# Softmax in slot-by-head rows, one accumulation for both outputs, and loads in order of use, in a fused attention and gated-MLP kernel

## The chip, the core and the metric

The kernel runs on one core of a Trainium2 chip. The metric is the device time of one launch in microseconds (us), as the median of several runs. A core has a matrix engine (TensorE, PE in the profile, with its weight loads listed apart as PEld), a vector engine (VectorE, DVE), a scalar engine (ScalarE, ACT) and a general engine (GpSimd, POOL). SyncE (SP) only issues transfers (DMAs). Each engine works through its own list of instructions in order, and engines wait for each other through semaphores. Matrix results go to PSUM, and other data lie in SBUF.

## The reference

One layer norm feeds two branches, which are added to the input. Sequence 2048, width 640, 32 heads of 20, and an attention window of 8 keys at distances 0, 2, ..., 14.

```
xn = layernorm(x)
q, k, v = split_heads(xn @ wqkv)                      # 640 -> 3*640
logits[s, w] = (q[s] . k[s - 2*w]) * scale            # w = 0..7, -1e9 where s - 2*w < 0
attn = softmax(logits, over w)
o[s] = sum_w attn[s, w] * v[s - 2*w]
out = x + o @ wo + ((xn @ w_gate) * (xn @ w_up)) @ w_down   # 640 -> 1536 -> 640
```

`wo` is the output projection. The softmax runs over eight slots per token and head. Data are bf16.

## The kernel before

The 2048 tokens are cut into four chunks of 512, and each chunk into four tiles of 128 tokens. In what follows "slot" is the window index w.

`proj_head(c)` (L153) loads the chunk's four x tiles from SP (L160), takes their statistics on DVE (`bn_stats` over five pieces of 128, L165; `bn_aggr`, L166), gets 1/std from one square root on ACT (L169) and one reciprocal on DVE (L172) for the whole chunk, and normalises each tile (L176). PE transposes each tile into `pst` (L186) and ACT copies it to `xnT_c` (L189). Then come 50 matmuls of 512 columns for q and k (L205, cast by ACT to `qT_c` and `kT_c`, L213 and L215) and 40 matmuls of 320 columns for v (L225, cast at L232). v goes to `vD` in DRAM (L233), since the window needs rows of v shifted against the partitions.

`prodlog(c)` (L238) makes the logits. DVE multiplies q with k shifted by 2w, one product `pw` per slot and half chunk (L250), and PE sums over the 20 features of each head with the 0/1 matrix `Ek`: 20 matmuls per group of four slots, placed side by side in the array, so that partition 32*j + h of `lps` holds slot j of head h (L259). ACT copies `lps` to `Lsb` in f32 (L268). `pw` has four buffers, so the next four products wait until PE has summed the last four.

`attn_core(c)` (L271) works tile by tile. It loads `v8`, eight shifted copies of v (L280), and transposes the logits to tokens-by-(slot, head) with two f32 PE transposes into `atp` (L283). Softmax follows in that layout: maximum (L299), difference (L302), exp on ACT (L305), sum (L307), reciprocal (L309), weight `a16` (L311). Then one large product `prod` = v8 * a16 (L316), a tree of three additions (L323, L325, L327) to `o16`, a transposition back (L330) and a copy to `oT_c` (L333). Tile 0 adds a mask first (L293 to L295).

`glu(c)` (L336) has 12 steps of 10 matmuls of 512 columns (L343, L352), two ACT casts (L360, L362) and one DVE product `hT_c` (L363). After them w_down gives `psB` (96 matmuls of 320 columns, L372), and DVE adds the residual x into `ob_c` (L379). `out_A(c)` (L387) multiplies `oT_c` with `wo` into `psA` (40 matmuls, L397), and DVE adds `ob_c` (L404) before the store from POOL's queue (L410).

All weights are loaded from POOL's queue: q and k first (L88), then v in five pieces whose buffers two ACT copies at a time must free (L94, L102), with the gate, up and down weights between them, and wo in 20 pieces (L143). The 10 first x tiles are issued by SP at the same time.

The program text runs projections of chunks 0 and 1, logits of chunk 0, and then per chunk: attention, GLU, projection of c+2, logits of c+1, output. A scheduler turns this text into one fixed list per engine, with instructions of neighbouring stages interleaved. The lists are fixed before the run, so an instruction whose input is late holds up everything behind it on its engine.

Of the kernel before, what the change touches and what calls it, by code (L numbers as in the profile page):

```python
# [15 lines left out]
def kernel(  # L16
# [35 lines left out]
    assert Dh % JL == 0 and Dh == JL * KT  # L52
    assert W * H == 2 * P

    TH = 256
    assert CS % TH == 0
    NTH = CS // TH

    if D <= 512:
        NSPL = [(0, D)]  # L60
    else:
        nspl = (D + 511) // 512
        assert D % nspl == 0
        NSPL = [(i * (D // nspl), D // nspl) for i in range(nspl)]

# [16 lines left out]
    wg = wpool.tile([P, KT, F], dt.bfloat16, name="wg")
    wu = wpool.tile([P, KT, F], dt.bfloat16, name="wu")
    wd = wpool.tile([P, FT, D], dt.bfloat16, name="wd")

    ident_bf = const.tile([P, P], dt.bfloat16, name="ident_bf")
    make_identity(nc, ident_bf[:])
    nc.gpsimd.dma_start(  # L88
        out=wqk[:], in_=A_wqkv[:, 0 : 2 * D].rearrange("(i p) f -> p i f", p=P)
    )  # L90
    st_tiles = []
    for i in range(KT):
        st = apool.tile([P, D], dt.bfloat16, name="st", tag="v8")
        nc.gpsimd.dma_start(  # L94
            out=st[:], in_=A_wqkv[i * P : (i + 1) * P, 2 * D : 3 * D]
        )
        st_tiles.append(st)
    nc.gpsimd.dma_start(out=wg[:], in_=B_w_gate.rearrange("(i p) f -> p i f", p=P))
    nc.gpsimd.dma_start(out=wu[:], in_=B_w_up.rearrange("(i p) f -> p i f", p=P))
    nc.gpsimd.dma_start(out=wd[:], in_=B_w_down.rearrange("(f p) d -> p f d", p=P))  # L100
    for i in range(KT):
        nc.scalar.copy(  # L102
            out=wvp[:, i, :].rearrange("p (j h) -> p j h", j=Dh, h=H),
            in_=st_tiles[i][:].rearrange("p (h j) -> p j h", h=H, j=Dh),
        )

    ident_f32 = const.tile([P, P], dt.float32, name="ident_f32")
    make_identity(nc, ident_f32[:])
    Ek = const.tile([P, KT, H], dt.bfloat16, name="Ek")
    for i in range(KT):  # L110
        et = apool.tile([P, D], dt.float32, name="et", tag="prod", bufs=1)
        nc.gpsimd.memset(et[:], 0.0)
        nc.gpsimd.tensor_copy(et[:, i * P : (i + 1) * P], ident_f32[:])
        e32 = apool.tile([P, H], dt.float32, name="e32", tag="m")
        nc.vector.reduce_sum(
            e32[:], et[:].rearrange("p (h j) -> p h j", h=H, j=Dh), AX.X
        )
        nc.vector.tensor_copy(Ek[:, i, :], e32[:])
# [34 lines left out]
    def proj_head(c):  # L153
# [3 lines left out]
        for ttl in range(CH):  # L157
# [6 lines left out]
            for g in range(KT):  # L164
                nc.vector.bn_stats(stats[:, g, :], x_t[:, g * P : (g + 1) * P])  # L165
# [288 lines left out]
```

## Time and profile before

| what | value |
|---|---|
| median of 6 runs | 332.79 us (331.89 to 334.89) |
| the profiled execution: its time | 333.7 us |
| its span (first to last instruction) | 331.9 us |
| granted PE clock, mean | 0.995 |
| transfers | 41.00 MB, 124 GB/s over the span |
| chain of waits, share by engine | DVE 31%, issue 26%, PE 22%, DMA 11%, ACT 5% |

How to read it: PE and DVE are the two loaded engines, and the chain of waits that ended last alternates between them. "Issue" is time in the chain in which the engine waited for nothing that the profile shows; here it stands mostly for PE or DVE working through its list while another engine's chain is followed. Matmuls are pipelined, so their busy time is not a pace: the pace of a group is the distance between the starts of two groups, divided by the count.

### The profile page before, as it was taken

What the parts mean: (1) busy time and instruction counts of PE and PEld (TensorE: products, weight loads), DVE (VectorE), ACT (ScalarE), POOL (GpSimd) and SP (SyncE); (2) the same over time, 40 slices, a digit from 0 to 9 for tenths busy, and PEclk for the clock granted to TensorE, in tenths of its full rate; (3) what the DMA queues carried; (4) which work ended last, traced back from release to release, by engine and by line L of the source; (5) the groups of instructions that cost most, each with busy time, mean ns of one, the idle gap of its engine ahead of it and who ended that gap; (6) DMA issues with size and microseconds to landing.
All of it is one profiled execution on the core that took longest, in us unless ns stands there. A gap on an engine that the chain in (4) does not pass through costs nothing.

```text
span 331.9 us, 5073 instructions
## 1 busy us (share of the span) xinstructions
PE 286.8 (86%) x1896; PEld 154.5 (47%) x1896; DVE 243.2 (73%) x452; ACT 134.0 (40%) x237; POOL 40.7 (12%) x84
## 2 busy tenths in 40 slices
PE   0139979799999889999999999999999799999990
PEld 0114544434446545544446646544446454445760
DVE  4352662678989895599889830798989797899861
ACT  1146654354651257245551255145541005553100
POOL 4022387000000100010000100010000111000111
PEclk9999999999999999999999999999999999999998
DMA  7828779310146625122346601115235711540011
GB/s 249 343 79 293 269 213 307 109 41 2 29 129 182 187 75 169 69 79 81 98 140 181 189 28 41 59 61 155 86 98 157 206 52 41 158 131 30 20 61 41
DMA packets 26922, 41.00 MB, mean 124 GB/s; under 512 B 3554, under 2 KB 24048, under 8 KB 26896
## 3 DMA queue, kind: packets, MB, share of 16 engines
q1 hardware_dynamic: 23040, 26.22, 25.9%
q0 software_dynamic: 3856, 14.44, 13.0%
q8 instruction: 15, 0.25, 0.3%
q14 instruction: 11, 0.09, 0.1%
HBM read 35.39 MB, written 5.26 MB: 122 GB/s over the span
## 4 chain that ended last, share of the span: by engine, by line
DVE 31%; issue 26%; PE 22%; DMA 11%; ACT 5%; POOL 2%; SPq 1%; POOLq 0%; DVEq 0%; ACTq 0%
DVE prod L316 9%; DMA x_t<-in_A_x_dram 6%; PE psqk L205 5%; PE psA L397 4%; PE lps L259 3%; DVE hT_c L363 3%; DMA xr<-in_A_x_dram 3%; PE psu L352 2%; PE psg L343 2%; DVE stats L165 2%; PE psv L225 2%; DVE ssum L307 2%; DVE ob_c L379 1%; DMA v_723<-vD 1%; DVE pw L250 1%
## 5 line engine op out<-in xcount | busy, mean ns | idle before, releaser
L250 DVE TENSOR_TENSOR pw<-qT_c,kT_c 128x1280 bf16<-128x1280 bf16 x64 | 49.0, 815 | 25.2 <-PE lps L259 25.2
L352 PE MATMUL psu<-xnT_c,wu 128*128 128x512 bf16 x240 | 61.3, 379 | 0.5 <-ACT gs L360 0.5
L343 PE MATMUL psg<-xnT_c,wg 128*128 128x512 bf16 x240 | 61.3, 379 | 0.0
L372 PE MATMUL psB<-wd,hT_c 128*128 128x320 bf16 x384 | 55.3, 299 | 1.8 <-DVE hT_c L363 1.6
L205 PE MATMUL psqk<-xnT_c,wqk 128*128 128x512 bf16 x200 | 46.6, 394 | 5.9 <-ACT xnT_c L189 5.9
L372 PEld LDWEIGHTS <-hT_c 128*128 128x128 bf16 x384 | 37.0, 98 | 18.4 <-DVE hT_c L363 4.1
L360 ACT CAST gs<-psg 128x512 bf16<-128x512 f32 x48 | 28.2, 587 | 26.4 <-PE psg L343 25.2
L362 ACT CAST us<-psu 128x512 bf16<-128x512 f32 x48 | 28.1, 586 | 20.2 <-PE psu L352 20.1
L352 PEld LDWEIGHTS <-wu 128*128 128x128 bf16 x240 | 23.2, 98 | 26.9 <-issue 1.1
L343 PEld LDWEIGHTS <-wg 128*128 128x128 bf16 x240 | 22.9, 98 | 26.9 <-issue 1.3
L205 PEld LDWEIGHTS <-wqk 128*128 128x128 bf16 x200 | 20.2, 101 | 31.2 <-issue 10.2
L333 ACT COPY oT_c<-pso 128x640 bf16<-128x640 bf16 x16 | 11.1, 692 | 58.1 <-PE pso L330 58.1
L165 DVE BATCH_NORM_STATS2 stats<-x_t 128x6 f32<-128x128 bf16 x80 | 16.8, 273 | 23.3 <-DMA x_t<-in_A_x_dram 23.3
L368 POOL DMA_DIRECT2D xr<-in_A_x_dram x16 | 8.7, 541 | 173.9 <-DVE ob_c L379 171.2
L397 PE MATMUL psA<-wo_perm,oT_c 128*128 128x320 bf16 x160 | 26.1, 301 | 0.0
L225 PE MATMUL psv<-wvp,xnT_c 128*128 128x320 bf16 x160 | 22.7, 299 | 2.2 <-ACT kT_c L215 1.6
L186 PE MATMUL pst<-ident_bf,xn_t 128*128 128x128 bf16 x80 | 7.4, 243 | 18.7 <-DVE xn_t L176 18.5
L259 PE MATMUL lps<-pw,Ek 128*32 128x256 bf16 x320 | 20.9, 276 | 2.3 <-DVE pw L250 2.3
L363 DVE TENSOR_TENSOR hT_c<-gs,us 128x512 bf16<-128x512 bf16 x48 | 19.9, 414 | 2.0 <-ACT us L362 2.0
L225 PEld LDWEIGHTS <-xnT_c 128*128 128x128 bf16 x160 | 15.6, 98 | 9.2 <-issue 2.6
L379 DVE TENSOR_TENSOR ob_c<-psB,xr 128x320 bf16<-128x320 f32 x32 | 15.3, 485 | 4.1 <-DMA xr<-in_A_x_dram 2.1
L410 POOL DMA_DIRECT2D out_dram<-osb x16 | 8.7, 544 | 78.5 <-DVE osb L404 78.5
(172 smaller groups left out, 304.9 us busy)
## 6 DMA issues: line engine op xcount, KB each, us to landing
x_t<-in_A_x_dram SPq DMA_DIRECT2D x16, 160.0 KB, 3.0
vD<-v_t SPq DMA_DIRECT2D x16, 160.0 KB, 1.9
xr<-in_A_x_dram POOLq DMA_DIRECT2D x16, 160.0 KB, 3.3
out_dram<-osb POOLq DMA_DIRECT2D x16, 160.0 KB, 2.1
wg<-in_B_w_gate_dram POOLq DMA_DIRECT2D x1, 1920.0 KB, 11.9
wu<-in_B_w_up_dram POOLq DMA_DIRECT2D x1, 1920.0 KB, 8.5
wd<-in_B_w_down_dram POOLq DMA_DIRECT2D x1, 1920.0 KB, 8.5
wqk<-in_A_wqkv_dram POOLq DMA_DIRECT2D x1, 1600.0 KB, 8.9
```

The source lines that it names most:

```text
L205: nc.tensor.matmul(ps[:], lhsT=wqk[:, i, r * D + j * P : r * D + (j + 1) * P], rhs=xnT_c[:, i, :], start=(i == 0), stop=(i == KT - 1),)
L225: nc.tensor.matmul(ps[:, 0:nsz], lhsT=xnT_c[:, i, tcols(ttl)], rhs=wvp[:, i, n0 : n0 + nsz], start=(i == 0), stop=(i == KT - 1),)
L250: nc.vector.tensor_tensor(pt[:], qT_c[:, :, hh * TH : (hh + 1) * TH], kT_c[:, :, off : off + TH], ALU.mult,)
L259: nc.tensor.matmul(lps[H * j : H * (j + 1), hh * TH : (hh + 1) * TH], lhsT=Ek[:, i, :], rhs=pw[j][:, i, :], start=(i == 0), stop=(i == KT ...
L316: nc.vector.tensor_tensor(prod[:].rearrange("p w (j h) -> p w j h", j=Dh, h=H), v8[:].rearrange("p w (j h) -> p w j h", j=Dh, h=H), a16[:, ...
L343: nc.tensor.matmul(psg[:], lhsT=wg[:, i, f * P : (f + 1) * P], rhs=xnT_c[:, i, :], start=(i == 0), stop=(i == KT - 1),)
L352: nc.tensor.matmul(psu[:], lhsT=wu[:, i, f * P : (f + 1) * P], rhs=xnT_c[:, i, :], start=(i == 0), stop=(i == KT - 1),)
L360: nc.scalar.copy(gs[:], psg[:])
L362: nc.scalar.copy(us[:], psu[:])
L363: nc.vector.tensor_tensor(hT_c[:, f, :], gs[:], us[:], ALU.mult)
L372: nc.tensor.matmul(psB[:, 0:nsz], lhsT=hT_c[:, f, tcols(ttl)], rhs=wd[:, f, n0 : n0 + nsz], start=(f == 0), stop=(f == FT - 1),)
L397: nc.tensor.matmul(psA[:, 0:nsz], lhsT=oT_c[:, g, tcols(ttl)], rhs=wo_perm[:, g, n0 : n0 + nsz], start=(g == 0), stop=(g == KT - 1),)
```

## The change

It rewrites the kernel's body with the same tiling and the same stage order in steady state. Its parts:

- **Softmax.** `weights(c)` takes the exp straight from `lps` on ACT, in the slot-by-head rows and without subtracting a maximum, into `e` (bf16). The mask is a 0/1 product on the first 16 columns of chunk 0. `attend` transposes with a matmul against `selb`, which holds two identities and, between them, a 0/1 block that sums the four slots of a head: two matmuls of 160 columns give the transposed values and, in 32 shared columns, the sum. DVE takes the reciprocal from PSUM and one product to `a16`. The additions of the tree are done in place.
- **Logits** by whole chunk: `pw` has 2560 elements instead of 1280, and there are half as many.
- **Norm.** Statistics over two pieces of 320; 1/std per tile on POOL (add, then power -0.5); no square root on ACT.
- **One accumulation.** `finish(c, ttl)` accumulates 12 matmuls for w_down and 5 for wo in one PSUM tile and adds the residual once. All of it comes after the logits of c+1.
- **Loads** all from SP's queue, in order of use: x, wq, wk, wv, first halves of gate and up, x of chunk 1, second halves, down, wo. The v weights are permuted by POOL (three pieces) and ACT (two).
- **Start.** Logits of chunk 0 stand before the projection of chunk 1, and the q/k matmuls of chunk 0 run in halves of 256 columns. PSUM pools are 4 + 2 + 2 banks instead of 5 + 2 + 1; `ps_tr`, with two, holds `pst`, `eT` and `pso`.

```diff
+    load_x(0)
+    nc.sync.dma_start(out=wqk[:, :, 0:D], in_=wqkv_r[:, :, 0:D])
+    nc.sync.dma_start(out=wqk[:, :, D : 2 * D], in_=wqkv_r[:, :, D : 2 * D])
+    nc.sync.dma_start(out=wst[:], in_=wqkv_r[:, :, 2 * D : 3 * D])
...
+    for i in range(KT):
+        eng = nc.gpsimd.tensor_copy if i % 2 == 0 else nc.scalar.copy
+        eng(
+            out=wvp[:, i, :].rearrange("p (j h) -> p j h", j=Dh, h=H),
+            in_=wst[:, i, :].rearrange("p (h j) -> p j h", h=H, j=Dh),
+        )
...
+            nc.gpsimd.tensor_scalar(rstd[:], mv[:, 1:2], EPS, None, op0=ALU.add)
+            nc.gpsimd.tensor_tensor(rstd[:], rstd[:], mhalf[:], ALU.pow)
...
+                pt = apool.tile([P, KT, CS], BF, name="pw", tag="pw", bufs=4)
...
+            nc.scalar.activation(e[:, g, :], lps[:], ACT.Exp, scale=scale)
...
+        eT = ps_tr.tile([P, 2 * (P + H)], F32, name="eT", tag="tr")
+        nc.tensor.matmul(
+            eT[:, 0 : P + H], lhsT=e[:, 0, tcols(ttl)], rhs=selb[:, 0 : P + H],
+            start=True, stop=False, skip_group_check=True,
+        )
+        nc.tensor.matmul(
+            eT[:, P : 2 * P + H], lhsT=e[:, 1, tcols(ttl)], rhs=selb[:, P : 2 * P + H],
+            start=False, stop=True, skip_group_check=True,
+        )
+        rs = apool.tile([P, H], F32, name="rs")
+        nc.vector.reciprocal(rs[:], eT[:, P : P + H])
...
+        nc.vector.tensor_tensor(prod[:, 0:4, :], prod[:, 0:4, :], prod[:, 4:8, :], ALU.add)
+        nc.vector.tensor_tensor(prod[:, 0:2, :], prod[:, 0:2, :], prod[:, 2:4, :], ALU.add)
...
+    def finish(c, ttl):
...
+            for g in range(KT):
+                nc.tensor.matmul(
+                    ps[:, 0:N2], lhsT=oT[:, g, :], rhs=wo_perm[:, g, n0 : n0 + N2],
+                    start=False, stop=(g == KT - 1),
+                )
+            nc.vector.tensor_tensor(
+                osb[:, n0 : n0 + N2], ps[:, 0:N2], xr[:, n0 : n0 + N2], ALU.add
+            )
...
+    proj(0, halves=2)
...
+    weights(0)
+    proj(1)
...
+        glu(c)
         if c + 2 < NCH:
-            proj_head(c + 2)
+            load_x(c + 2)
+            proj(c + 2)
         if c + 1 < NCH:
-            prodlog(c + 1)
-        out_A(c)
+            weights(c + 1)
+        for ttl in range(CH):
+            finish(c, ttl)
```

How the lists move is shown at three places. First ACT's list at the start of the program, before:

```order
L169 ACT_TABLE_LOAD
L169 ACTIVATE rstd<-mvc,eps_t 128x4
L189 COPY xnT_c<-pst 128x5x128 x3
L102 COPY wvp<-st 128x640 x2
L189 COPY xnT_c<-pst 128x5x128
L213 CAST qT_c<-psqk 128x512
```

and with the change (`wst` is the staged v weight):

```order
L160 ACT_TABLE_LOAD
L160 COPY xnT<-pst 128x5x128
L133 COPY wvp<-wst 128x640 x2
L160 COPY xnT<-pst 128x5x128 x3
L187 CAST qT<-psqk 128x256 x5
L187 CAST kT<-psqk 128x256 x5
```

The two copies of the v weight now stand behind the first transposed tile instead of the third. Second, DVE's list where chunk 0's logits meet chunk 1's normalisation, before:

```order
L198 COPY kT_c<-kT_c 128x5x14
L250 TENSOR_TENSOR pw<-qT_c,kT_c 128x1280 x4
L115 TENSOR_REDUCE e_117<-et 128x32
L176 TENSOR_SCALAR xn_t<-x_t,mvc,rstd 128x640
L118 CAST Ek<-e_117 128x32
L176 TENSOR_SCALAR xn_t<-x_t,mvc,rstd 128x640
```

and with the change:

```order
L223 TENSOR_TENSOR pw<-qT,kT 128x2560 x4
L169 COPY kT<-kT 128x5x14
L223 TENSOR_TENSOR pw<-qT,kT 128x2560 x4
L153 TENSOR_SCALAR xn_t<-x_t,mv,rstd 128x640 x2
L234 TENSOR_TENSOR e<-e,vmask 128x2x16
L254 RECIPROCAL rs<-eT 128x32
```

Chunk 1's last two normalised tiles now stand behind all eight products of chunk 0's logits; before, they stood behind a quarter of them. Third, DVE's list for one attention tile inside the GLU of chunk 1 (its second tile), before:

```order
L299 TENSOR_REDUCE m<-atp 128x32
L302 TENSOR_TENSOR d<-atp,m 128x256
L363 TENSOR_TENSOR hT_c<-gs,us 128x512
L307 TENSOR_REDUCE ssum<-d 128x32
L309 RECIPROCAL rs<-ssum 128x32
L311 TENSOR_TENSOR a_1657<-d,rs 128x256
L316 TENSOR_TENSOR prod<-v_1636,a_1657 128x5120
L363 TENSOR_TENSOR hT_c<-gs,us 128x512
L323 TENSOR_TENSOR p_1661<-prod 128x2560
L363 TENSOR_TENSOR hT_c<-gs,us 128x512
L325 TENSOR_TENSOR p_1663<-p_1661 128x1280
```

and with the change:

```order
L254 RECIPROCAL rs<-eT 128x32
L256 TENSOR_TENSOR a_1524<-eT,rs 128x256
L265 TENSOR_TENSOR prod<-v_1510,a_1524 128x5120
L303 TENSOR_TENSOR hT<-gs,us 128x512
L271 TENSOR_TENSOR prod<-prod 128x2560
L303 TENSOR_TENSOR hT<-gs,us 128x512
L272 TENSOR_TENSOR prod<-prod 128x1280
L274 TENSOR_TENSOR o_1530<-prod 128x640
L303 TENSOR_TENSOR hT<-gs,us 128x512
```

The maximum, the difference and the sum are gone, and three GLU products stay between the steps of a tile. All four attention tiles still run inside the 12 GLU steps of their chunk.

More of the change, by code (lines that the diff above doesn't have):

```diff
@@ L47 @@
     CH = 4
-    assert NT % CH == 0
     NCH = NT // CH
@@ L51 @@
     JL = P // H
[L52 to L64, printed above, removed]
+    N2 = D // 2
+    FH = F // 2
     const = ctx.enter_context(tc.tile_pool(name="const", bufs=1))
@@ L82 @@
[L82 to L118, printed above, removed]
```

476 lines of the change are left out of this document (205 added, 271 removed).

## The prediction

> **What bounds the kernel now.** I read the page's totals first, then the busy time by stage, with borders that I set at the first q/k matmul, at the first gate matmul of chunks 1, 2 and 3, and at PE's last matmul.
>
> ```profile
> span 331.9 us, 5073 instructions
> PE 286.8 (86%) x1896; PEld 154.5 (47%) x1896; DVE 243.2 (73%) x452; ACT 134.0 (40%) x237; POOL 40.7 (12%) x84
> ...
> 0.00:23.20 23.20, 2.50 (x21) 2.04 (x22) 11.27 (x55) 6.59 (x8) 4.56 (x12) 1.00 0.64 229
> 23.20:144.90 121.70, 113.78 (x757) 59.56 (x757) 84.67 (x169) 57.79 (x106) 23.06 (x49) 1.00 0.46 145
> 144.90:218.00 73.10, 70.28 (x476) 38.18 (x475) 53.19 (x83) 32.11 (x57) 4.32 (x9) 1.00 0.32 100
> 218.00:272.40 54.40, 51.30 (x344) 27.70 (x343) 48.97 (x75) 18.77 (x33) 4.11 (x9) 1.00 0.40 121
> 272.40:324.00 51.60, 48.94 (x305) 26.99 (x302) 44.17 (x70) 18.71 (x33) 3.52 (x7) 1.00 0.24 74
> 324.00:331.90 7.90, 0.00 (x0) 0.00 (x0) 0.90 (x3) 0.00 (x0) 1.08 (x2) 0.81 0.13 44
> ```
>
> The columns are the stretch, its length, then busy us and instructions of PE, PEld, DVE, ACT and POOL, granted clock, DMA share and GB/s. The reader is to see that PE stands still for 23 us at the start, and is then the engine that is nearly always busy. DVE comes next: 49.0 of 54.4 us in the third stretch. Next I took PE's pace from the timeline.
>
> ```profile
> 154.61 1.24 PE L352 MATMUL psu<-xnT_c,wu 128*128 128x512 bf16 x5
> 155.69 1.24 PE L343 MATMUL psg<-xnT_c,wg 128*128 128x512 bf16 x5
> ...
> 178.75 8.86 PE L372 MATMUL psB<-wd,hT_c 128*128 128x320 bf16 x64
> ...
> 157.71 0.45 PE L330 MATMUL pso<-ident_bf,o_1627 128*128 128x128 bf16 x5 [0.35 <-DVE o_1627 L327]
> ...
> 188.70 0.72 PE L186 MATMUL pst<-ident_bf,xn_t 128*128 128x128 bf16 x10
> ...
> 261.57 0.73 PE L259 MATMUL lps<-pw,Ek 128*32 128x256 bf16 x20
> ```
>
> Five matmuls of 512 columns take 155.69 - 154.61 = 1.08 us, 0.216 each; 320 columns take 8.86/64, about 0.137 without the last one's drain. A chunk's stream is then: GLU 120 x 0.216 = 25.9; down 96 x 0.137 = 13.2; wo 40 x 0.137 = 5.5; q/k 10.9; v 40 x 0.137 = 5.4; logits 4 x 0.65 = 2.6; transposes of x 1.3 and of o 1.2; f32 transposes about 1.4. Sum 67.4 us. The stretch from 144.9 to 218.0 holds exactly one such set, so 73.1 - 67.4 = 5.7 us of it is waiting. The next has no projection (49.8), leaving 4.6; the last also no logits (47.2), leaving 4.4. The kernel is bound by PE's stream of some 270 us, plus the start, the tail and waits. A change helps only where it shortens the start, the stream or the waits. The waits of the steady part come from DVE's attention tile, whose rows follow (chain of waits first, then groups: busy us and mean ns of one, idle before).
>
> ```profile
> 161.56 2.82 DVE prod L316
> ...
> 171.61 2.83 DVE prod L316
> ...
> L307 DVE TENSOR_REDUCE ssum<-d 128x32 f32<-128x256 f32 x16 | 9.5, 595 | 3.0 <-ACT d L305 2.9
> L299 DVE TENSOR_REDUCE m<-atp 128x32 f32<-128x256 f32 x15 | 6.4, 424 | 6.8 <-PE atp L283 6.8
> L302 DVE TENSOR_TENSOR d<-atp,m 128x256 f32<-128x256 f32 x15 | 6.3, 422 | 0.4
> L295 DVE TENSOR_TENSOR d<-d,m 128x256 f32<-128x256 f32 x1 | 0.4, 419 | 0.0
> L309 DVE RECIPROCAL rs<-ssum 128x32 f32<-128x32 f32 x16 | 5.6, 350 | 0.4
> L363 DVE TENSOR_TENSOR hT_c<-gs,us 128x512 bf16<-128x512 bf16 x48 | 19.9, 414 | 2.0 <-ACT us L362 2.0
> L323 DVE TENSOR_TENSOR p_1661<-prod 128x2560 bf16<-128x2560 bf16 x1 | 1.5, 1484 | 0.0
> L325 DVE TENSOR_TENSOR p_1663<-p_1661 128x1280 bf16<-128x1280 bf16 x1 | 0.8, 817 | 0.0
> L327 DVE TENSOR_TENSOR o_1665<-p_1663 128x640 bf16<-128x640 bf16 x1 | 0.5, 481 | 0.0
> L379 DVE TENSOR_TENSOR ob_c<-psB,xr 128x320 bf16<-128x320 f32 x32 | 15.3, 485 | 4.1 <-DMA xr<-in_A_x_dram 2.1 <-PE pst L186 1.3 <-PE psB L372 0.6
> ```
>
> A tile takes DVE 171.61 - 161.56 = 10.05 us. Four of them (40.2) stand beside PE's GLU, 6 us of transposes and most of `psB`: 25.9 + 13.2 + 2.6 = 41.7. The two engines are matched, and each exchange costs PE a few tenths.
>
> **The change, part by part.** The sum is made on the profiled execution (span 331.9 us), stage by stage.
>
> *Start.* These rows show it before.
>
> ```profile
> 10.30 0.29 DVE L165 BATCH_NORM_STATS2 stats<-x_t 128x6 f32<-128x128 bf16 x1 [4.01 <-DMA x_t<-in_A_x_dram]
> 18.67 1.25 PE L186 MATMUL pst<-ident_bf,xn_t 128*128 128x128 bf16 x10 [4.50 <-DVE xn_t L176]
> 20.01 2.54 ACT L102 COPY wvp<-st 128x640 bf16<-128x640 bf16 x2
> 23.20 13.57 PE L205 MATMUL psqk<-xnT_c,wqk 128*128 128x512 bf16 x50 [3.28 <-ACT xnT_c L189]
> 28.62 7.65 PEld L205 LDWEIGHTS <-wqk 128*128 128x128 bf16 x36 [0.20 <-issue]
> 46.55 10.95 PE L205 MATMUL psqk<-xnT_c,wqk 128*128 128x512 bf16 x50 [1.54 <-ACT xnT_c L189]
> ...
> L189 ACT COPY xnT_c<-pst 128x640 bf16<-128x640 bf16 x16 | 10.3, 714 | 6.4 <-PE pst L186 6.4
> ...
> 0.00:8.30 8.30, 0.00 (x0) 0.00 (x0) 3.41 (x19) 1.28 (x1) 3.64 (x10) 1.00 0.78 249
> 8.30:16.60 8.30, 1.25 (x10) 0.99 (x10) 2.99 (x13) 1.58 (x3) 0.00 (x0) 1.00 0.85 343
> ...
> v_723<-vD SPq DMA_DIRECT2D x8, 160.0 KB, 4.5
> ```
>
> Before, the x tiles share the engines with the weights, and PE's first q/k matmul starts at 23.2. With the change x comes first, but ACT's list puts two v-weight copies behind the first transposed tile, so everything waits for the staged v weight. In front of it lie 4 x tiles (0.66 MB), wq and wk (1.64) and itself (0.82): 3.1 MB. The first 16.6 us moved 249 and 343 GB/s x 8.3 us = 4.9 MB, in some 14.6 us without the first two: 336 GB/s. That gives 2.0 + 9.3, and about 0.7 for two residual tiles that POOL issues early: 12.0 us (bounds: 10.5 without sharing, 14.4 at 249 GB/s). Then 2.54 for the two copies, 0.7 for the next `xnT`, 0.7 for the last transposes: q/k starts at 15.9, a gain of **7.3**. That SP issues larger transfers is not shown; bounded by the 10 and 14 above. POOL's three v copies have until the v matmuls, 13 us later. SP's list is in order too: the v writes and the first `v8` loads now stand behind all weights, 10.5 MB or 33 us at this rate; v is ready at 32 to 36, and with 4.5 for the eight loads `v8` lands near 43, before its first use at 47. If the rate is 249 instead, it lands near 49 and that tile is 2 us late.
>
> *Up to the GLU of chunk 1* (before: 23.2 to 144.9). q/k of chunk 0 takes 13.6 again (100 matmuls of half the width, same stream), v 5.4: 34.9. Here the new order has nothing to put under chunk 0's logits: eight products of 2560 elements at 1.48 (the row of L323, same shape) run from 29.7 in two groups of 5.9 with a 1.2 us sum after each, since four buffers hold one group. The last normalised tiles of chunk 1 stand behind them, so its q/k starts at 46.3: 11.4 us with 3.7 us of PE work in them. That wait also costs pace. PE took 13.57 for 50 matmuls after waits of 4.50 and 3.28 us, the first 14 of them in 28.62 - 23.20 = 5.4 us, but 10.95 after a wait of 1.54. Here the longest wait is near 6, so I take 13.6: 59.9, and 65.3 after v. DVE then needs 8.1 for the next four products and four statistics from 60.3 (its copy of the k halo waits for the last k cast), and 28.5 for three tiles, 12 GLU products, statistics and normalisation: 97. PE's 27 of GLU fit under it. q/k of chunk 2 starts at 98.6; 16.3 for q/k and v, 1.2 logits, 136 x 0.137 = 18.6 for the joined outputs: 134.7. The stage takes 118.8 instead of 121.7: gain **2.9**.
>
> *Chunks 1 to 3.* A tile on DVE is 0.35 + 0.42 (the price of L302, also PSUM, 256 elements) + 2.82 + 1.48 + 0.82 + 0.48 + 3 x 0.41 = 7.6, less 0.5 for overlapping starts, plus about 0.4 for the round over PE at its end: 7.5. PE's share per tile is 33 x 0.216 + 0.45 + 0.15 = 7.7, so PE is ahead by a hair, and I give it 1 us of waits per GLU. The f32 transposes become two bf16 matmuls of 160 columns (bounds 0.06, as a transposition, to 0.14 as 320 columns): 0.8 us less per chunk. `ob_c` goes: 8 x 0.485 per chunk off DVE, hidden by PE's `psB` before, so worth nothing by itself. Chunk 1: DVE's fourth tile ends 30.3 after the start, then five ACT copies of 0.7 in a row (two banks hold `pso` and the `pst` tiles) to 33.9, 16.3, 1.2, 18.6, 0.3: 70.3 instead of 73.1, gain **2.8**. Chunk 2: 25.9 + 1.2 + 0.6 + 2.4 + 18.6 + 1.0 = 49.7 instead of 54.4, gain **4.7**. Chunk 3, without logits: 47.3 instead of 51.6, gain **4.3**. The exp costs ACT what the copy to `Lsb` cost; statistics, 16 exps and the sqrt tables go from engines with room.
>
> *Tail.* The last tile was one of four that queued for stores:
>
> ```profile
> 324.29 0.89 DVE L404 TENSOR_TENSOR osb<-psA,ob_c 128x320 bf16<-128x320 f32 x2 [0.28 <-DMA out_dram<-osb]
> ...
> 325.47 0.54 POOL L410 DMA_DIRECT2D out_dram<-osb  x1 [0.62 <-DVE osb L404]
> ```
>
> From PE's end to the span's end it was 7.9 us; tiles now end 4.6 us apart, so only 0.5 for the addition and the 6.5 from 325.4 on remain: gain **0.9**.
>
> Sum: 7.3 + 2.9 + 2.8 + 4.7 + 4.3 + 0.9 = 22.9, span 309.0. The profiled run's time is 333.7, 1.8 above its span and 0.9 above the median of 332.79: 309.0 + 1.8 - 0.9 = 309.9, so **310 us**.
>
> **The power on POOL.** No row shows it. One-element rows bound it:
>
> ```profile
> L438 POOL MEMSET const-float32-1.0<- 128x1 f32 x1 | 0.1, 99 | 0.0
> L112 POOL MEMSET et<- 128x640 f32 x5 | 3.2, 640 | 6.1 <-DVE e_117 L115 5.0 <-DVE e_123 L115 1.1
> ```
>
> Four additions and four powers are 0.8 to 5.1 us behind the statistics, which end near 7.2, and one 0.5 us DMA issue. I take 0.8, the row of the same size. The wait for the v weight covers all up to about 10.8; at 5.1 the first transposed tile is 2.4 late, and the time 312. [...]
>
> **Rivals.**
> 1. *PE does not pay the slow pace at chunk 1's q/k, and the v weight lands at 10.5.* For it: short sums and transposes lie in the wait. Against: 1.25 us of transposes at 18.67 did not help. 310 - 2.6 - 1.5 = 306. Chance 0.15.
> 2. *DVE stays the bound of the GLU.* If the strided reads from PSUM cost what the strided sum does (595 ns) and the round at a tile's end stays uncovered, a tile is 8.5, 0.8 above PE's, over 16 tiles 13 us: 323. For it: 7.5 against 7.7 is a thin margin. Against: GLU products stand ready in the gaps. Chance 0.13.
> 3. [...] Chance 0.08.
> 4. *Slower: the additions in place lose pace.* If reading and writing the same tile halves DVE's pace, they take 2.8 and 1.5 instead of 1.48 and 0.82, 2.0 more per tile. It decides once a tile passes PE's 7.7: 9.5 leaves 1.8 x 16 = 29 us of waits, 339. Against: in tile 0 the difference is written in place (L295) in 419 ns, and elsewhere not in place (L302) in 422; both are f32, so the bf16 pace is not shown. Chance 0.05.
> 5. *The change does not do what it says*: the softmax saving is hidden by PE anyway, and only start and tail gain: 332.8 - 8.2 = 325. Chance 0.03.
>
> **How the numbers follow.** The forecast, 310 (305 to 318 with its bounds), has 0.56. The range takes in rivals 1 to 3: 302 to 324, leaving out rivals 4 and 5 and the far ends, under 0.2. Within 0.5% is about what a measurement of this kernel can tell from no change. Faster by more has 0.92, slower by more 0.05 (rival 4), the rest 0.03.
>
> **What would show it.** First q/k matmul at 16, waiting for ACT (the v copies); chunk 1's q/k at 46, waiting for ACT behind `pw`, and 13.6 long; GLU of chunks 1, 2, 3 starting near 135, 205 and 255; `prod` every 7.5 to 7.7 us; in-place additions of 1.48 and 0.82; PE's end near 302. It is wrong if PE waits for `o` more than 1 us per tile, if the transfer of the v weight ends after 14.5, or if DVE waits for `v8`.

## The result and the profile after

| | before | after |
|---|---|---|
| median, us | 333.05 (330.59 to 336.02, 20 runs) | 309.52 (308.38 to 314.02, 10 runs) |
| ratio to before | 1 | 0.9298, 95% interval 0.9266 to 0.9329 |
| profiled execution and its span, us | 333.70, 331.9 | 310.36, 308.7 |

The first two rows are the page's totals of the kernel after. Below them stands the busy time by stage, with borders at the same events as before: the first q/k matmul, the first gate matmul of chunks 1, 2 and 3, and PE's last matmul.

```profile
span 308.7 us, 4647 instructions
PE 277.5 (90%) x1786; PEld 157.1 (51%) x1786; DVE 196.0 (64%) x277; ACT 123.5 (40%) x221; POOL 45.6 (15%) x92
...
0.00:18.15 18.15, 2.42 (x20) 2.02 (x21) 5.64 (x17) 5.66 (x6) 12.23 (x38) 1.00 0.91 301
18.15:133.80 115.65, 110.21 (x728) 64.37 (x727) 74.95 (x113) 53.69 (x106) 20.49 (x31) 0.97 0.49 152
133.80:204.65 70.85, 67.65 (x438) 37.43 (x435) 44.54 (x54) 29.59 (x52) 4.30 (x8) 1.00 0.34 103
204.65:255.95 51.30, 50.49 (x327) 27.22 (x326) 37.80 (x48) 17.93 (x30) 4.30 (x8) 1.00 0.43 129
255.95:303.50 47.55, 46.66 (x285) 26.04 (x282) 32.62 (x44) 16.67 (x28) 3.77 (x7) 1.00 0.27 80
303.50:308.70 5.20, 0.10 (x1) 0.00 (x0) 0.49 (x1) 0.00 (x0) 0.54 (x1) 0.72 0.08 32
```

DVE lost 47 us of work (243.2 to 196.0), PE only 9. The span shrank by 23.2 us: 5.05 at the start, 6.05 up to the GLU of chunk 1, 2.25, 3.1 and 4.05 in the three chunks behind it, and 2.7 at the tail. What PE still waits for in chunk 1, at a tile's end, shows in its timeline (start, busy us, line, idle before):

```profile
141.34 0.45 PE L277 MATMUL pso<-selb,o_1500 128*128 128x128 bf16 x5 [0.24 <-DVE o_1500 L274]
149.03 0.45 PE L277 MATMUL pso<-selb,o_1530 128*128 128x128 bf16 x5 [0.20 <-DVE o_1530 L274]
156.93 0.45 PE L277 MATMUL pso<-selb,o_1560 128*128 128x128 bf16 x5 [0.19 <-DVE o_1560 L274]
164.84 0.45 PE L277 MATMUL pso<-selb,o_1590 128*128 128x128 bf16 x5 [1.37 <-DVE o_1590 L274]
166.07 0.44 PE L159 MATMUL pst<-selb,xn_t 128*128 128x128 bf16 x5 [0.50 <-ACT oT L279]
167.99 0.23 PE L245 MATMUL eT<-selb,e 128*128 128x160 bf16 x1 [0.27 <-ACT xnT L160]
168.59 10.95 PE L179 MATMUL psqk<-xnT,wqk 128*128 128x512 bf16 x50 [0.36 <-ACT xnT L160]
```

Tiles end 7.7 to 7.9 us apart, and PE loses 0.2 us at three of them and 1.4 at the last, behind which the next projection stands. The groups (busy us, mean ns of one, idle before) price what the trace of before could not:

```profile
L271 DVE TENSOR_TENSOR prod<-prod 128x2560 bf16<-128x2560 bf16 x16 | 23.7, 1483 | 0.0
L151 POOL TENSOR_TENSOR rstd<-rstd,mhalf 128x1 f32<-128x1 f32 x16 | 15.3, 967 | 1.0
L272 DVE TENSOR_TENSOR prod<-prod 128x1280 bf16<-128x1280 bf16 x16 | 13.1, 817 | 0.0
```

### The profile page after: what moved, and what is told of

Read it like the earlier page. It is cut to its first block, busy times and chain, and to the rows that moved or that the text cites. A ratio compares the mean times of both kernels' runs of the same rounds, so it can differ in the third digit from the quotient of the medians.

```text
span 308.7 us, 4647 instructions
## 1 busy us (share of the span) xinstructions
PE 277.5 (90%) x1786; PEld 157.1 (51%) x1786; DVE 196.0 (64%) x277; ACT 123.5 (40%) x221; POOL 45.6 (15%) x92
## 4 chain that ended last, share of the span: by engine, by line
PE 48%; DVE 30%; DMA 9%; SPq 4%; issue 3%; ACT 3%; POOLq 0%; POOL 0%; DVEq 0%
PE psqk L179 15%; DVE prod L265 13%; DVE pw L223 5%; DVE prod L271 4%; PE psv L197 4%; DMA wst<-in_A_wqkv_dram 3%; DVE hT L303 3%; PE lps L227 3%; SPq L243 3%; DVE prod L272 2%; ACT xnT L160 2%; PE psu L294 2%; PE psg L288 1%; PE pso L277 1%; PE pst L159 1%
## 5 line engine op out<-in xcount | busy, mean ns | idle before, releaser
L223 DVE TENSOR_TENSOR pw<-qT,kT 128x2560 bf16<-128x2560 bf16 x32 | 46.0, 1481 | 26.8 <-ACT v_t L202 14.8
L288 PE MATMUL psg<-xnT,wg 128*128 128x512 bf16 x240 | 60.4, 379 | 0.0
L294 PE MATMUL psu<-xnT,wu 128*128 128x512 bf16 x240 | 60.3, 379 | 0.0
L179 PE MATMUL psqk<-xnT,wqk 128*128 128x512 bf16 (+1 forms) x250 | 46.6, 351 | 0.8 <-ACT xnT L160 0.8
L316 PEld LDWEIGHTS <-hT 128*128 128x128 bf16 x384 | 37.0, 98 | 16.9 <-issue 2.2
L288 PEld LDWEIGHTS <-wg 128*128 128x128 bf16 x240 | 23.2, 98 | 26.1
L271 DVE TENSOR_TENSOR prod<-prod 128x2560 bf16<-128x2560 bf16 x16 | 23.7, 1483 | 0.0
L197 PE MATMUL psv<-wvp,xnT 128*128 128x320 bf16 x160 | 22.4, 299 | 0.0
L146 DVE BATCH_NORM_STATS2 stats<-x_t 128x6 f32<-128x320 bf16 x32 | 14.0, 467 | 12.1 <-DMA x_t<-in_A_x_dram 12.1
L303 DVE TENSOR_TENSOR hT<-gs,us 128x512 bf16<-128x512 bf16 x48 | 19.8, 413 | 0.1
L197 PEld LDWEIGHTS <-xnT 128*128 128x128 bf16 x160 | 15.7, 98 | 6.5
L321 PEld LDWEIGHTS <-oT 128*128 128x128 bf16 x160 | 15.6, 98 | 6.5 <-issue 0.6
```

The lines of the kernel that those rows point to most:

```text
L179: nc.tensor.matmul(ps[:, 0:n], lhsT=wqk[:, i, r * D + j * P : r * D + (j + 1) * P], rhs=xnT[:, i, t0 : t0 + n], start=(i == 0), stop=(i == ...
L197: nc.tensor.matmul(ps[:, 0:N2], lhsT=xnT[:, i, tcols(ttl)], rhs=wvp[:, i, n0 : n0 + N2], start=(i == 0), stop=(i == KT - 1),)
L223: nc.vector.tensor_tensor(pt[:], qT[:], kT[:, :, off : off + CS], ALU.mult)
L271: nc.vector.tensor_tensor(prod[:, 0:4, :], prod[:, 0:4, :], prod[:, 4:8, :], ALU.add)
L288: nc.tensor.matmul(pg[:], lhsT=wg[:, i, f * P : (f + 1) * P], rhs=xnT[:, i, :], start=(i == 0), stop=(i == KT - 1),)
L294: nc.tensor.matmul(pu[:], lhsT=wu[:, i, f * P : (f + 1) * P], rhs=xnT[:, i, :], start=(i == 0), stop=(i == KT - 1),)
```

## The experiments

The table holds what all of them gave, in us. The ratio is to the kernel before, run beside each; its median there lay between 331.6 and 333.8, so medians of different rows can be 2 us apart for that alone, and ratios compare better. First q/k and GLU 1 (the first gate matmul of chunk 1) are starts in the profiled execution; chunk 1 and chunk 2 run from one GLU's start to the next, chunk 3 to PE's end.

| kernel | median | ratio | first q/k | GLU 1 | chunk 1 | chunk 2 | chunk 3 |
|---|---|---|---|---|---|---|---|
| before | 333.05 | 1 | 23.2 | 144.9 | 73.1 | 54.4 | 51.6 |
| after | 309.52 | 0.9298 | 18.2 | 133.8 | 70.8 | 51.3 | 47.6 |
| new softmax alone, in before | 325.49 | 0.9751 | 25.1 | 143.3 | 70.4 | 51.3 | 49.9 |
| shifted softmax, in after | 336.99 | 1.0089 | 16.9 | 145.0 | 83.5 | 52.2 | 49.3 |
| the same, down matmuls early | 321.60 | 0.9678 | 17.7 | 138.2 | 71.1 | 55.9 | 49.2 |
| two accumulations | 310.56 | 0.9297 | 18.8 | 133.8 | 71.2 | 51.8 | 47.3 |
| dose of 0.49 us a tile | 316.92 | 0.9456 | 18.7 | 134.8 | 76.5 | 51.1 | 47.6 |
| dose of 1.49 us a tile | 329.38 | 0.9860 | 19.4 | 138.7 | 82.0 | 52.3 | 47.9 |
| v copies on GpSimd | 305.67 | 0.9120 | 11.8 | 128.8 | 70.9 | 51.3 | 47.7 |
| projection first | 317.05 | 0.9493 | 17.1 | 143.3 | 67.7 | 51.6 | 47.7 |
| both | 317.12 | 0.9488 | 11.5 | 143.4 | 67.7 | 51.6 | 47.7 |
| half the GLU early | 325.74 | 0.9833 | 11.4 | 144.7 | 74.5 | 51.3 | 47.7 |
| the same, outputs early | 317.74 | 0.9571 | 12.1 | 129.7 | 80.6 | 51.3 | 47.7 |
| logits first, outputs early | 306.96 | 0.9249 | 11.6 | 128.7 | 70.6 | 51.0 | 47.7 |

### What the softmax is worth, and where

The new softmax alone, in the kernel before (loads, order and outputs as before):

```diff
-            nc.scalar.copy(Lsb[:, g, :], lps[:])
+            nc.scalar.activation(Lsb[:, g, :], lps[:], ACT.Exp, scale=scale)
...
+            nc.tensor.matmul(
+                eT[:, 0 : P + H], lhsT=Lsb[:, 0, tcols(ttl)], rhs=selb[:, 0 : P + H],
+                start=True, stop=False, skip_group_check=True,
+            )
+            nc.tensor.matmul(
+                eT[:, P : 2 * P + H], lhsT=Lsb[:, 1, tcols(ttl)], rhs=selb[:, P : 2 * P + H],
+                start=False, stop=True, skip_group_check=True,
+            )
...
```

> Edit: the kernel before with only the new softmax (exp and mask in slot rows, transposed and summed by two bf16 matmuls, reciprocal and product out of PSUM); loads, order, statistics, logit products and the two accumulations stay as before. Theory A (the parts add up as predicted: 3.3 us of waits and 0.8 us of f32 transposes per chunk): 333.5 - 16 = 317, 315 to 321. Theory B (the parts hang together: the softmax is worth the 27 us here that it is worth in the changed kernel): 304 to 309. Theory C (the softmax saving was hidden by PE in the kernel before, and the rest of the change is what gained): 328 to 331.

It took 325.49, ratio 0.9751 (0.9688 to 0.9815): faster by 7.7 us, between theories A and C. In chunks 1 and 2 it gained 2.7 and 3.1, as much as the whole change did there (2.3 and 3.1), and in chunk 3 1.7 of 4.05. Nothing else in the change is needed for what chunks 1 and 2 gained.

The opposite edit, the shifted softmax put back into the kernel after:

```diff
-            nc.scalar.activation(e[:, g, :], lps[:], ACT.Exp, scale=scale)
+            nc.scalar.copy(e[:, g, :], lps[:])
...
+            nc.vector.reduce_max(m[:], eT[:].rearrange("p (w h) -> p h w", w=W, h=H), AX.X)
+            nc.vector.tensor_tensor(
+                d[:], L3, m[:, None, :].to_broadcast([P, W, H]), ALU.subtract
+            )
+        nc.scalar.activation(d[:], d[:], ACT.Exp, scale=scale)
...
+        nc.vector.reduce_sum(ssum[:], d[:].rearrange("p w h -> p h w"), AX.X)
```

> Edit: the changed kernel with the softmax of the kernel before put back: f32 logits copied from PSUM, transposed by f32 identity, max, difference, exp, sum, reciprocal and product per token tile; one buffer instead of two for d, twelve instead of fourteen for hT, the rest of the change stays. Theory A (the softmax is what the GLU stages gained): a tile on DVE takes 0.42 + 0.42 + 0.60 more plus two more exchanges (exp on ScalarE 0.35 each way), so some 9.5 to 10 us instead of 7.7; PE waits 1.8 to 2.2 per tile in 15 of 16 tiles and the f32 transposes cost 0.8 a chunk: 309.5 + 28 = 337 at the most, less what the last tile of a chunk hides under the down matmuls, 4 to 6 a chunk: 318 to 325. Rival (PE's stream hides DVE's saving, and only the transposes count): 309.5 + 3 = 312.5.

It took 336.99, 0.9% slower than the kernel before (1.0089, 1.005 to 1.0127). So the softmax is worth 27.5 us in the new order (26 by the ratios) and 7.7 in the old one, and the rest of the change without it loses some 3 us. This kernel also has one buffer for `d` and 12 instead of 14 for `hT`; what that costs was not measured by itself. The expected 318 to 325 missed the time; only the "337 at the most" came near, and for another reason, since the loss isn't spread over the tiles. Chunks 2 and 3 lose 0.9 and 1.7, chunk 1 loses 12.7. PE's timeline of this kernel there:

```profile
174.92 0.45 PE L287 MATMUL pso<-selb,o 128*128 128x128 bf16 x5 [0.51 <-DVE o L284]
177.53 0.38 PE L233 MATMUL lps<-pw,Ek 128*32 128x512 bf16 x1 [1.39 <-DVE pw L229]
...
188.86 0.71 PE L287 MATMUL pso<-selb,o 128*128 128x128 bf16 x5 [3.81 <-DVE o L284]
...
193.28 10.95 PE L185 MATMUL psqk<-xnT,wqk 128*128 128x512 bf16 x50 [0.42 <-ACT xnT L166]
```

Tiles end 9.9 us apart here. Up to the third, GLU matmuls stand beside them; beside the fourth there is nothing but logit sums that wait for DVE themselves, since the products of the next chunk were put between that tile's steps. From 175.2 to 193.3 PE is busy for 8.4 of 18.1 us. In the kernel before, 13 us of down matmuls lay at this place; the one accumulation moved them behind the projection. To see whether that is the cause, the down matmuls went back to right behind the GLU, into a PSUM tile of their own, with the shifted softmax kept (and two buffers instead of three for `xnT`):

```diff
         glu(c)
+        for ttl in range(CH):
+            down(c, ttl)
```

> Edit: the kernel with the shifted softmax put back (337.0), and in it the down matmuls moved from the output stage to right behind the GLU, into a PSUM tile of their own and a bf16 tile ob, as the kernel before had them; two buffers instead of three for xnT. In the traces the shifted softmax costs 12 us each in chunks 0 and 1, where the next projection stands right behind the last attention tile, and only 0.9 and 1.7 in chunks 2 and 3. Theory A (the rest of the change took the cover away: without down matmuls between the GLU and the projection nothing lies beside the last tile): 13.2 us of matmuls cover most of it in chunks 0 and 1 again, 9 to 12 us each: 313 to 319. Theory B (the cost has another cause, for instance the two PSUM banks that all transposes share): 333 to 338.

It took 321.60: 15.4 us of the 27.5 came back (14 of 26 by the ratios). Chunk 1 fell from 83.5 to 71.1, as theory A has it; GLU 1 starts 6.7 earlier. Chunk 2, which needed no cover, lost 3.7, and so the total is 2.6 above the range. PE's timeline now:

```profile
168.77 1.67 PE L326 MATMUL psB<-wd,hT 128*128 128x320 bf16 x11 [0.39 <-DVE hT L313]
180.81 0.45 PE L287 MATMUL pso<-selb,o 128*128 128x128 bf16 x5 [0.59 <-DVE o L284]
...
185.26 10.95 PE L185 MATMUL psqk<-xnT,wqk 128*128 128x512 bf16 x49 [0.24 <-ACT xnT L166]
```

The fourth o is still late, 42.6 us behind the GLU's start against 43.9 without the early down matmuls, but now 13 us of down matmuls lie beside it. So for chunk 1 this is shown: the new order took away the cover that a slow attention tile needs, and the short softmax is what makes that order possible. Some 12 of the 27.5 us did not come back. They lie ahead of GLU 1, in chunk 2 and in chunk 3 (4.4, 4.6 and 1.7 us more than in the changed kernel), and their cause stays open.

### Two accumulations, and room on DVE

Two PSUM tiles in the output stage, at its new place, with 32 additions more:

```diff
+            nc.vector.tensor_tensor(ob[:], psB[:, 0:N2], xr[:, n0 : n0 + N2], ALU.add)
...
-            nc.vector.tensor_tensor(
-                osb[:, n0 : n0 + N2], ps[:, 0:N2], xr[:, n0 : n0 + N2], ALU.add
-            )
+            nc.vector.tensor_tensor(osb[:, n0 : n0 + N2], psA[:, 0:N2], ob[:], ALU.add)
```

> Edit: in the output stage the down and the attention products go to two PSUM tiles again, the first added to the residual into a bf16 tile ob, the second to ob: 32 more additions of 0.49 us on DVE (15.7 us). Theory (the prediction's price, nothing: DVE waits 1.8 us for PE before each output addition): 309.5, 308.5 to 311. Rival (four PSUM tiles shared by twice as many accumulations, and additions ahead of the products of the next chunk's logits, make PE wait): 1 to 4 us a chunk, 313 to 325.

310.56, ratio 0.9297 (0.9256 to 0.9338) beside 0.9298: no difference can be told. The joined sum itself is worth nothing, as the prediction priced it. With the slow softmax its place mattered, as shown above; with the short one the old place was not tried.

A dose of DVE work in each attention tile (k is 1 or 4; the values written are not used):

```diff
+        nc.vector.tensor_tensor(prod[:, 4 : 4 + k, :], prod[:, 0:k, :], prod[:, 0:k, :], ALU.add)
         o16 = apool.tile([P, D], BF, name="o16")
```

> Edit: one more DVE addition of 640 elements in every attention tile (0.49 us, in the free upper half of prod, ahead of the last addition); the output is the same. Theory (DVE's tile and PE's stretch are matched at 7.7, with 0.2 to 0.4 us to spare in each): 0 to 0.3 us a tile over 15 tiles, 309.5 to 314. Rival (PE's stream hides DVE, which is busy for only 64% of the span): no change, 309 to 310.5.

> Edit: the same with 2560 elements (1.49 us a tile). Theory (matched engines, 0.2 to 0.4 us to spare): 1.1 to 1.3 us a tile over 15 tiles, 16 to 20 us: 325 to 330; where the fixed lists also place the next chunk's logit products between the steps of a chunk's last tile, as in the kernel with the softmax of before, some 5 us more. Rival (PE's stream hides DVE): under 312.

316.92 and 329.38, ratios 0.9456 (0.9382 to 0.953) and 0.986 (0.9813 to 0.9906); one of the four runs with the small dose took 312.91. The totals, 7.4 and 19.9 us more (5.3 and 18.7 by the ratios), look like a price per tile, but the table tells against this reading. Chunks 2 and 3 hide even the large dose to within 1.0 us. Chunk 1 pays 5.7 and 11.1, more than its four doses (2.0 and 6.0), and from GLU to GLU chunk 0 pays 0.3 and 4.3, less than its doses. The large dose fell into its range, but not by the sum over tiles that gave the range: that is luck. PE's timeline with the small dose, in chunk 1:

```profile
168.18 0.59 PE L227 MATMUL lps<-pw,Ek 128*32 128x512 bf16 x1 [3.55 <-DVE pw L223]
168.98 0.72 PE L278 MATMUL pso<-selb,o 128*128 128x128 bf16 x5 [0.22 <-DVE o L275]
```

The fourth tile's transposition comes 34.2 us after the GLU's start instead of 31.0, later than four doses make it. The dose has also changed the fixed lists: a logit product of the next chunk now stands between the steps of the fourth tile on DVE, and its sum stands ahead of the transposition on PE, where it waits 3.55 us; in the kernel without the dose that sum comes behind. The q/k matmuls after it then take 12.3 instead of 10.8. So the last tile of chunk 1 has no room, while chunks 2 and 3, which have no projection behind their GLU, have some. The doses don't tell the added work apart from the changed lists. The small dose fell outside its range by what chunk 1 paid.

### The start

```diff
-        eng = nc.gpsimd.tensor_copy if i % 2 == 0 else nc.scalar.copy
+        eng = nc.gpsimd.tensor_copy
```

> Edit: all five v-weight copies on GpSimd instead of three there and two on ScalarE; nothing else. Theory A (the start is set by the two ScalarE copies, which stand ahead of the second to fourth transposed tile and wait for the v weight at 14.4 us): ScalarE then copies the four tiles in a row from 9.9, the first q/k matmul moves from 18.15 to about 12.4, the five copies end near 21, before the v matmuls at 25.4, and the whole chain of chunk 0 moves 5.8 us; what DVE needs from outside (the v rows read back, 49.4 us now) comes no later than that chain less 1 us. Time about 304.5 (5 less than the changed kernel's 309.5). Theory B (behind the start the loads are the bound: the v rows still land near 49, because all weights stand ahead of them): q/k starts at 12.4, but DVE's first product of attention stays near 49.8 and the GLU of chunk 1 starts less than 2 us earlier than 133.8. Time 308 to 309.5.

305.67, ratio 0.912 (0.9044 to 0.9195), faster than the changed kernel. PE's timeline of this kernel:

```profile
9.18 1.25 PE L159 MATMUL pst<-selb,xn_t 128*128 128x128 bf16 x10 [9.18 <-POOL rstd L151]
10.67 1.29 PE L159 MATMUL pst<-selb,xn_t 128*128 128x128 bf16 x10 [0.25 <-ACT xnT L160]
11.76 11.60 PE L179 MATMUL psqk<-xnT,wqk 128*128 128x256 bf16 x100
```

DVE's timeline, at its first product of attention:

```profile
46.61 2.83 DVE L265 TENSOR_TENSOR prod<-v,a 128x5120 bf16<-128x5120 bf16 x1 [1.72 <-DMA v<-vD]
```

q/k started 6.4 earlier and ran 1.6 shorter, so v ended 8.0 earlier, and 5.0 of that reached GLU 1. The other 3 went where theory B looked, in part: DVE's logit products began only at 27.1, behind statistics of chunk 1, and the first product of attention waited 1.72 for v, which theory A had excluded. Theory A holds in the main.

### The pause at chunk 0's logits

Between chunk 0's v and chunk 1's q/k lie 12 us. PE is busy for 7.4 of the 11.7 us from 37.0 to 48.7, with sums and transpositions that the prediction priced at 3.7 us at full pace. Five kernels tried to fill this pause. First the old order of the two steps, alone and with the v copies moved:

```diff
+    proj(1)
     weights(0)
-    proj(1)
```

> Edit: the projection of chunk 1 is emitted before the logits of chunk 0, as it was in the kernel before; nothing else. Theory A (the 12 us between the v matmuls of chunk 0 and the q/k of chunk 1, with 3.7 us of matrix work in them, are time lost for good): q/k of chunk 1 starts near 38 instead of 48.7, the GLU of chunk 0 near 58 instead of 65.9, that of chunk 1 near 126.5; time about 302. Theory B (the wait only moves: from 49 to 92 us DVE has no gaps, and it starts its first tile of attention no sooner): GLU of chunk 0 starts near 58 but PE waits for o in it or for the normalised tiles behind it, 5 us or more; GLU of chunk 1 starts at 131 to 134; time 307 to 310.

> Edit: both edits together, the v-weight copies on GpSimd and the projection of chunk 1 ahead of the logits of chunk 0. If each gain is independent (theory A of both): 309.5 - 5 - 7.5 = 297. If the order of projection and logits only moves a wait, the time is that of the copies alone, within 1.5 us: 303 to 306. If the read-back of v behind the weights bounds the stage: 307 to 309.5.

317.05 and 317.12, slower than the changed kernel by 7.5 (6.5 by the ratios); none of the theories allowed for that. So the new order of the two steps, which the prediction took for a cost, is worth that much in the changed kernel. The GLU of chunk 0 started at 57.3 instead of 65.9, as both said, but that of chunk 1 at 143.3 instead of 133.8. DVE's timeline ahead of attention, and in the last attention tile of chunk 0:

```profile
51.44 0.18 DVE L169 COPY kT<-kT 128x70 bf16<-128x70 bf16 x1 [6.44 <-ACT kT L187]
...
89.09 1.48 DVE L223 TENSOR_TENSOR pw<-qT,kT 128x2560 bf16<-128x2560 bf16 x1
90.50 0.35 DVE L254 RECIPROCAL rs<-eT 128x32 f32<-128x32 f32 x1
90.76 1.43 DVE L223 TENSOR_TENSOR pw<-qT,kT 128x2560 bf16<-128x2560 bf16 x1
92.11 0.41 DVE L256 TENSOR_TENSOR a<-eT,rs 128x256 bf16<-128x256 f32 x1
92.44 1.48 DVE L223 TENSOR_TENSOR pw<-qT,kT 128x2560 bf16<-128x2560 bf16 x1
93.83 2.82 DVE L265 TENSOR_TENSOR prod<-v,a 128x5120 bf16<-128x5120 bf16 x1
96.57 1.48 DVE L223 TENSOR_TENSOR pw<-qT,kT 128x2560 bf16<-128x2560 bf16 x1
```

On PE the second group of chunk 0's logit sums now stands behind the projection (at 56.15), so DVE begins attention at 62.3 instead of 48.6; on the way it waits 6.44 us, at its copy of the k halo, for the last k cast of chunk 1. By the third tile the delay has shrunk to 5.2 us. Then four logit products of the next chunk stand ahead of and between the steps of the tile for which PE waits, and it ends at 101.4 instead of 92.4. So theory B is right that DVE starts its first tile no sooner, but not that DVE has no gaps (it is busy for 46.6 of the 52.4 us from 49.0 to 101.4), and the fixed list adds to the delay.

Then half of chunk 0's GLU as filling, on top of the v copies, without and with the outputs of chunk 0 ahead of the projection of chunk 2:

```diff
+    glu(0, 0, FT // 2)
     weights(0)
     proj(1)
...
-        glu(c)
+        glu(c, FT // 2 if c == 0 else 0)
```

> Edit: all v-weight copies on GpSimd (305.7), and the first six of the twelve GLU blocks of chunk 0 emitted ahead of chunk 0's logits. Theory A (PE's waits in the logits, 28.7 to 44.3 us, are lost for good): 13 us of GLU matmuls fill them, q/k of chunk 1 starts near 45.5 and the GLU of chunk 1 10 us earlier than 128.8: 296 to 298. Theory B (DVE is the bound up to the last attention tile of chunk 0: products, tiles and statistics in a row from 26 to 87 us): the fourth o comes no earlier, PE waits for it behind the shortened GLU, GLU of chunk 1 within 2 us of 128.8: 304 to 307.

> Edit: as the one before, and the output stage of chunk 0 emitted ahead of the projection of chunk 2, so that its matmuls lie beside the attention tiles that are left. Theory A and B of the run before both allow a gain here, of different size: by A the early GLU has it all already and this adds nothing (296 to 298 in both); by B only this one gains, since 18.6 us of output matmuls stand where PE would wait for the fourth o: GLU of chunk 1 at 117 to 122 instead of 128.8, time 294 to 299, against 304 to 307 without it.

325.74 and 317.74, both worse than without the filling; each is some 19 us above the highest time that a theory gave for it. DVE's timeline of the first:

```profile
26.45 5.64 DVE L223 TENSOR_TENSOR pw<-qT,kT 128x2560 bf16<-128x2560 bf16 x4
...
37.81 0.43 DVE L303 TENSOR_TENSOR hT<-gs,us 128x512 bf16<-128x512 bf16 x1 [5.62 <-ACT us L301]
...
49.41 5.69 DVE L223 TENSOR_TENSOR pw<-qT,kT 128x2560 bf16<-128x2560 bf16 x4
```

PE is full from 33.6 to 48.3, but the first logit sums stand behind the GLU in its list and DVE's second four products behind the GLU's products: they start at 49.4 instead of 34.3, and every attention tile is late with them. In the second kernel the outputs beside the tiles win most of that back up to GLU 1 (129.7), and chunk 1 loses 9.7 us again (80.6 against 70.9): there, too, logit products stand between the steps of the last tile on DVE (at 163.3, 166.1 and 168.3). Last, the GLU behind the logits, so that sums go first, and outputs ahead of the projection in all chunks:

```diff
     weights(0)
+    glu(0, 0, FT // 2)
     proj(1)
...
-        glu(c)
+        glu(c, FT // 2 if c == 0 else 0)
+        if c + 1 < NCH:
+            weights(c + 1)
+        for ttl in range(CH):
+            finish(c, ttl)
         if c + 2 < NCH:
             load_x(c + 2)
             proj(c + 2)
-        if c + 1 < NCH:
-            weights(c + 1)
-        for ttl in range(CH):
-            finish(c, ttl)
```

> Edit: all v-weight copies on GpSimd (305.7); the first six GLU blocks of chunk 0 emitted behind the logits of chunk 0, so that they fill PE's gaps without standing ahead of the logit sums; and in every chunk the next chunk's logits and this chunk's output stage emitted ahead of the projection two chunks on. Theory A (DVE sets the pace up to the last attention tile of chunk 0, and PE's 12.5 us of waits between 28.8 and 128.8 can be filled as long as no DVE work is pushed back): q/k of chunk 1 starts near 46, the fourth o of chunk 0 comes no later than 90, PE has output matmuls beside it, and the GLU of chunk 1 starts at 114 to 120 instead of 128.8; the chunk after it gains 1 to 2 us more, since no projection stands right behind its last tile: 305.7 - 10 = 296, 293 to 299. Theory B (any work put into PE's gaps pushes back a sum that DVE waits for, as in the two runs with the early GLU): 306 to 318.

306.96, ratio 0.9249 (0.9196 to 0.9303), which is theory B's case; no gain over the v copies alone (0.912, 0.9044 to 0.9195). Two rows of PE show where: it waited 3 us before the early GLU, and q/k of chunk 1 started at 53.1 where theory A had 46.

```profile
33.01 0.38 PE L288 MATMUL psg<-xnT,wg 128*128 128x512 bf16 x1 [3.05 <-ACT v_t L202]
...
53.11 10.95 PE L179 MATMUL psqk<-xnT,wqk 128*128 128x512 bf16 x49 [0.30 <-ACT xnT L160]
```

The first transposition of e stands behind the early GLU too, so DVE begins attention at 52.9 instead of 44.1 and GLU 1 starts at 128.7, where it was. In all five kernels PE's pause was filled or moved, and DVE's chain up to the last attention tile of chunk 0 began later or ran longer. That this chain sets GLU 1 fits all of them, but was not tested by itself. An order that fills the pause without pushing that chain back was not found.

## Why the prediction was right

Time, range and main mechanism held: 310 against 309.52, span 309.0 against 308.7. That the total came so close is luck: the start and chunks 1 to 3 together gained 4.65 us less than their terms, the stage up to GLU 1 and the tail 4.95 us more. The terms:

- **Start**, 7.3 predicted, 5.05 measured. The step "12.0 us" for the v weight's landing was mis-sized; ScalarE's timeline has the copies begin at its upper bound, though not by the low rate that gave this bound:

```profile
14.47 2.56 ACT L133 COPY wvp<-wst 128x640 bf16<-128x640 bf16 x2 [3.88 <-DMA wst<-in_A_wqkv_dram]
```

  and PE's timeline what waited for them:

```profile
17.66 0.69 PE L159 MATMUL pst<-selb,xn_t 128*128 128x128 bf16 x5 [6.34 <-ACT xnT L160]
18.15 13.20 PE L179 MATMUL psqk<-xnT,wqk 128*128 128x256 bf16 x100
```

  The page's slices of 7.72 us give what was moved by then:

```profile
GB/s 202 376 370 347 120 238 229 270 110 148 138 150 76 0 80 17 79 82 171 173 169 171 2 54 31 87 85 172 170 170 172 42 83 93 170 126 3 42 47 40
```

  202 x 7.72 and 376 x 6.75 are 4.1 MB by 14.47 us, which is near the forecast's rate (329 GB/s from 2.0 us on, against 336), but not the 3.4 MB counted in front of it: what was issued behind it (gate and up weights, at 4.29 and 5.41) had taken part of the rate. That the copies on ScalarE are what held PE is shown by the edit that moved them.
- **The power on POOL** takes 0.53 us at the start (2.14 for four) and not 0.1, and lay under the wait for the v weight, as said: PE transposed the first tile at 9.14, and 6.34 us of waiting for the copies came behind it. With that wait gone, it is what the first transposition waits for (9.18). A power late enough to cost time in the changed kernel, for which rival 3 had its 0.08, is shown by no run: the first additions ran 0.47 us for two at 5.47, and the four powers ended at 10.15. Rival 3 falls.
- **Pace behind the pause**, 2.6 predicted on q/k of chunk 1. It took 11.3 where 13.6 was predicted and 10.9 is full pace (10.95 in chunk 1). The slow pace was there, but on the sums and transpositions before it. Stretches of PE alone (length, busy us, granted clock, DMA share, GB/s):

```profile
37.00:44.40 7.40, 3.49 (x37) 0.90 0.81 219
44.40:48.70 4.30, 3.88 (x30) 0.50 1.00 307
48.70:52.00 3.30, 3.30 (x13) 0.83 0.78 264
```

  So this half of rival 1 is what happened, though not its earlier v weight. The two errors, 2.25 late and 2.3 too slow, nearly cancel: GLU of chunk 0 at 65.9 against 65.3.
- **Up to GLU 1** then 68.0 against 69.4 from the GLU of chunk 0; start of GLU 1 133.8 against 134.7.
- **Chunks**: 70.85, 51.3 and 47.55 against 70.3, 49.7 and 47.3. The exp takes ACT 597 ns where the copy to `Lsb` took 586, as said. The 1.6 in chunk 2 lie among its output matmuls: from 234.09 to 255.81 PE takes 21.7 us, where 136 of them at 0.136 (17 take 2.31 us from 244.26 on), 17 sums in 1.2 and five transpositions in 0.3 make 20.0. The rest goes to three single logit sums between the output matmuls, for which the forecast had 0.06 us each. PE's timeline at the first, which waits 0.33 us and takes 0.31:

```profile
236.77 0.38 PE L227 MATMUL lps<-pw,Ek 128*32 128x512 bf16 x1 [0.33 <-DVE pw L223]
237.08 0.31 PE L321 MATMUL pso_2659<-wo_perm,oT 128*128 128x320 bf16 x1
```

- **Tile on DVE**: PE ahead "by a hair", tiles 7.7 to 7.9 apart, so rival 2 with its 8.5 falls. The doses cost time in chunks 0 and 1 alone. Rival 4 falls: additions in place ran 1483 and 817 ns, as those not in place (1484 and 817).
- **Rival 5** falls: the softmax gains 7.7 alone, and the change without it gains nothing. Its 325 would itself have been faster than before, so its 0.03 belonged with the 0.92 for faster.
- **The tail** took 5.2 and not 7.0: the last store ended 4.3 us behind its issue at 304.4, no longer 6.4.
- **Signs of being wrong**: all three were brushed. PE waited for `o` 0.2 us at most tiles, but 1.37 at the last of chunk 1; the v weight's copies began at 14.47, against 14.5; and DVE waited once for v, 0.40 us at the first product of attention (49.77).

What the prediction didn't see is that its parts don't add up: it priced the softmax by waits, gave the moved outputs no price and took the new order of logits and projection for a loss, each against the kernel before. The sum came out because all were there.

## What to carry to other kernels

Where a change joins or moves the matmuls that lie beside a slow tile, price the tile in the order that is left, since a saving that was worth 8 us can be worth 27 there. A pause of the busiest engine is worth filling only if no work of the engine that feeds it is pushed back (all five attempts here pushed some back, and none gained over the kernel it started from); look in the fixed lists for what stands between the steps of the last tile. Let a bandwidth estimate for the n-th transfer count some of what is issued behind it: here 4.1 MB had moved where 3.4 were counted.
